# Cross-covariance attention with a multiplicative feed-forward: last outputs that lag, softmax steps closer together, and the first q tile on another DMA queue

## The chip, the cores and the metric

The kernel runs on one core of one Trainium2 chip. The metric is the device time of one execution in microseconds (us). The profile's span leaves some 1.8 us of the measured time out.

## The reference, cut to what matters

```python
B, N, C = 4, 5824, 256                    # q, k, v: [B, N, C], f32; tau = 1
qn = q / (norm(q, axis=1) + 1e-6);  kn = k / (norm(k, axis=1) + 1e-6)
a  = softmax(kn.transpose(0, 2, 1) @ qn / tau)          # [B, 256, 256]
x  = (v @ a).reshape(B * N, C)
out = ((x @ w1) * (x @ w2)) @ w3 @ w_out                # w1, w2: 256 x 1024; w3: 1024 x 1024; w_out: 1024 x 256
```

The kernel never forms x. It folds the attention matrix of a batch into w1 and w2 (`Wf`), multiplies w3 by w_out once (`W_sb`), and then does for each 512 tokens and each of 8 slices: two products from v with `Wf` (a and b), a cast of a by ScalarE, a product a*b by VectorE, and an output product with `W_sb`.

## The kernel before: the parts that the change touches

TensorE works through batches `b`, chunks `c` of 512 tokens (the last one, "small", has 128 tokens and the 64 left over of a batch) and slices `j`. Everything for the next batch (scores, softmax, folds) hangs on an agenda of (time, work), whose clock counts TensorE's columns. `run_due` emits what is due, so a time on the agenda becomes a place in each engine's program.

```python
nc.scalar.preload_act_table_set("natural_log_exp_and_others")      # at the top
...
return (                                                # softmax of a batch after the first: (cost, time, work)
    [(0.0, 0.0, norms), (0.0, 6.0, k_row)]              # norms: all-reduce on GpSimd
    + [(0.0, 6.0 + 1.3 * i, lambda i=i: k_step(i)) for i in range(4)]
    ...
    + [(0.0, 11.3 + 1.3 * ct, lambda ct=ct: scale(ct)) for ct in range(CT)]
    + [(0.0, 12.0 + 1.3 * ct, lambda ct=ct: exps(ct)) for ct in range(CT)]
    + [(0.2, 16.5, sums)]
    + [(0.43, 17.5 + 1.1 * i, lambda i=i: fold(i)) for i in range(8)]
)
...
for nm in "kq":                                         # the first tiles, uncast
    raw[nm] = work.tile([P, half, C], F32, tag="o_sb", name=f"raw_{nm}", bufs=3)
    nc.sync.dma_start(out=raw[nm], in_=qk_main[nm, 0][0][:, :half, :])
    load_part(nm, 0, 0, half, PIECE)                    # the rest: GpSimd's casting loads
...
for jt in range(FT):
    at(26.0 + 1.2 * jt, 0.87, lambda jt=jt: w_unit(jt)) # w3 @ w_out; needs w3 turned by DMA
...
lag = LAG_END if b == B - 1 and c == NCH - 1 else LAG   # 5 or 2: outputs run behind a and b
while w_ready[0] and len(pend) > lag and npop < 2:
    emit_out(*pend.pop(0))
...
while pend:                                             # the end
    emit_out(*pend.pop(0))
```

In `emit_out` the small chunk of an odd batch has two output matmuls per slice, first the leftover rows of both batches, then the main rows. At the last slice ScalarE copies the main rows to SBUF and issues their store, and VectorE copies the leftover rows; the stores of their two halves go by SyncE and, at the very end, by ScalarE.

## Time and profile before

| | value |
|---|---|
| time, median of 3 runs | 571.08 us (570.57 to 572.03) |
| span of the profiled run | 569.5 us |
| TensorE busy, clock | 98%, 1.00 |
| last matmul starts | 565.36 us |
| from there to the end of the span | 4.10 us |

Read it in this order: which engine is busy, then whether its "busy" hides waiting, then where. The lines are in the prediction. One thing to know for its first group of lines: the GB/s of a casting load count the bf16 bytes that it writes (the list of DMA issues has 512 KB for eight tiles of q or k that come by a casting load, and the same 512 KB for four that come uncast). So 211 GB/s in the stage from 6 to 30 us and 418 GB/s of the uncast tiles at 3 us are the same rate of reading.

### The profile page before, as it was taken

The numbers are of one execution on the slowest core, as the hardware profiler recorded it, in microseconds if no ns is written. First come the engines' busy times: TensorE is split into PE (matmuls) and PEld (weight loads), VectorE is DVE, ScalarE is ACT, GpSimd is POOL, SyncE is SP. The second block draws the span as 40 slices with busy tenths as digits, with TensorE's granted clock in tenths as the row PEclk, the third lists the DMA queues.
The fourth block names the chain that finished last, engine by engine and source line by source line (L and its number), as shares of the span: only waits on it lengthen the run. The fifth ranks groups of instructions, "written<-read, shape, count | busy, mean of one in ns | idle before, by whom it ended". The sixth has DMA issues, their size and how long they took to land.

```text
span 569.5 us, 10098 instructions
## 1 busy us (share of the span) xinstructions
PE 558.9 (98%) x3755; PEld 354.9 (62%) x3755; DVE 375.7 (66%) x581; ACT 340.5 (60%) x627; POOL 77.2 (14%) x163
## 2 busy tenths in 40 slices
PE   8799999999999999999999999999999999999997
PEld 5664576776666666666666666666665656656665
DVE  1047645788966577887766567787866665565564
ACT  1057535777766577777675567777756554454453
POOL 4260013020220110121210111030120000000000
PEclk9999999999999999999999999999999999999999
DMA  9999989978455696595761495766740325221011
GB/s 213 211 175 208 168 170 233 225 171 195 112 147 120 132 194 147 98 184 128 148 148 73 95 217 121 155 120 121 184 112 39 85 74 148 63 70 68 38 73 58
DMA packets 75105, 77.45 MB, mean 136 GB/s; under 512 B 54193, under 2 KB 58801, under 8 KB 75057
## 3 DMA queue, kind: packets, MB, share of 16 engines
q0 software_dynamic: 15760, 38.93, 39.1%
q1 hardware_dynamic: 59072, 37.69, 22.3%
q8 instruction: 29, 0.48, 0.3%
q10 hardware_dynamic: 224, 0.20, 0.1%
q14 instruction: 20, 0.16, 0.1%
HBM read 78.91 MB, written 23.86 MB: 180 GB/s over the span
## 4 chain that ended last, share of the span: by engine, by line
PE 91%; DMA 6%; ACT 1%; DVE 1%; POOL 0%; issue 0%; ACTq 0%; POOLq 0%
PE o L519 28%; PE b L477 27%; PE a L477 27%; PE G L193 5%; DMA k<-in_k_dram 5%; PE fold L364 2%; DMA w3T<-w_wout 1%; PE w L643 1%; ACT kr L284 0%; ACT as L483 0%; PE quarter L390 0%; POOL k L112 0%; DVE s L318 0%; ACT e L323 0%; DVE abs L498 0%
## 5 line engine op out<-in xcount | busy, mean ns | idle before, releaser
L498 DVE TENSOR_TENSOR abs<-as,b 128x512 bf16<-128x512 bf16 x336 | 230.2, 686 | 138.0 <-ACT as L483 124.9
L483 ACT CAST as<-a 128x512 bf16<-128x512 f32 (+1 forms) x384 | 216.2, 563 | 173.4 <-DVE abs L498 87.1
L477 PEld LDWEIGHTS <-Wf 128*128 128x128 bf16 x1536 | 148.8, 98 | 101.7 <-issue 1.8
L477 PE MATMUL a<-vT,Wf 128*128 128x512 bf16 x704 | 209.4, 379 | 0.4 <-ACT Wf L399 0.4
L477 PE MATMUL b<-vT,Wf 128*128 128x512 bf16 x704 | 209.4, 379 | 0.0
L519 PE MATMUL o<-W_sb,abs 128*128 128x256 bf16 x1344 | 201.1, 273 | 0.0
L519 PEld LDWEIGHTS <-abs 128*128 128x128 bf16 x1344 | 131.4, 98 | 80.8
L202 DVE TENSOR_TENSOR acc<-acc,sq 128x1024 f32<-128x1024 f32 x66 | 80.4, 1219 | 0.7 <-ACT sq L190 0.7
L193 PE MATMUL G<-k,q 128*128 128x256 bf16 x276 | 49.6, 273 | 0.0
L190 ACT ACTIVATE sq<-q 128x512 f32<-128x512 bf16 x66 | 41.8, 634 | 0.0
L190 ACT ACTIVATE sq<-k 128x512 f32<-128x512 bf16 x66 | 41.6, 630 | 0.0
L465 POOL COPY gate_t<-abs 1x1 bf16<-1x1 bf16 x39 | 9.4, 241 | 170.1 <-DVE abs L498 168.8
L540 DVE COPY osb<-o 128x512 f32<-128x512 f32 x44 | 30.1, 684 | 0.9 <-PE o L519 0.9
L193 PEld LDWEIGHTS <-q 128*128 128x128 bf16 x276 | 27.0, 98 | 3.1
L539 ACT COPY osb<-o 128x512 f32<-128x512 f32 x44 | 25.8, 586 | 3.8 <-PE o L519 1.8
L469 POOL COPY gate_t<-vT 1x1 bf16<-1x1 bf16 x16 | 3.3, 208 | 162.5 <-DMA vT<-v 162.5
L112 POOL DMA_DIRECT2D q<-in_q_dram x28 | 15.1, 539 | 12.5 <-DMA k<-in_k_dram 5.5
L284 ACT ACTIVATE kr<-row 128x256 f32<-128x256 f32 x1 | 0.4, 384 | 26.0 <-PE row L272 26.0
L371 ACT ACTIVATE Wf<-fold,rs 128x512 bf16<-128x512 f32 x15 | 10.3, 688 | 9.0 <-PE fold L364 9.0
L488 DVE TENSOR_TENSOR left<-as,b 128x192 bf16<-128x192 bf16 x32 | 11.2, 353 | 5.7 <-ACT as L483 3.5
L364 PE MATMUL fold<-w,e 128*128 128x512 bf16 x56 | 14.7, 379 | 0.0
L498 DVE TENSOR_TENSOR abq<-as,b 128x512 bf16<-128x512 bf16 x16 | 10.8, 686 | 5.1 <-ACT as L483 4.6
(98 smaller groups left out, 241.8 us busy)
## 6 DMA issues: line engine op xcount, KB each, us to landing
out_dram<-osb SPq DMA_DIRECT2D x44, 512.0 KB, 3.6
k<-in_k_dram POOLq DMA_DIRECT2D x19, 512.0 KB, 8.6
v<-in_v_dram POOLq DMA_DIRECT2D x19, 512.0 KB, 5.2
q<-in_q_dram POOLq DMA_DIRECT2D x18, 512.0 KB, 6.6
w_wout<-in_moe_w_dram POOLq DMA_DIRECT2D x1, 2048.0 KB, 23.1
k<-in_k_dram POOLq DMA_DIRECT2D x4, 320.0 KB, 7.6
v<-in_v_dram POOLq DMA_DIRECT2D x4, 320.0 KB, 5.3
q<-in_q_dram POOLq DMA_DIRECT2D x3, 320.0 KB, 4.3
```

Source lines behind the costliest of these rows:

```text
L112: nc.gpsimd.dma_start(out=pieces[nm, n, pi][:, lo:hi, :], in_=qk_main[nm, n][0][:, pi * PIECE + lo : pi * PIECE + hi, :])
L190: nc.scalar.activation(out=dst[:, :, part, :], in_=src[:, o : o + 2, :], func=AF.Square)
L193: nc.tensor.matmul(G[:, ct, :], lhsT=qt[:, i, ct * P : (ct + 1) * P], rhs=kt[:, i, :], start=(pr == 0 and part == 0 and ct == 0), stop=(pr ...
L202: nc.vector.tensor_add(accs[n], accs[n], sqs[0])
L364: nc.tensor.matmul(m, lhsT=st["e"][:, c2, c1 * P : (c1 + 1) * P], rhs=w12[:, c2, w, lo:hi], start=(c2 == 0), stop=(c2 == CT - 1),)
L477: nc.tensor.matmul(t[:, :n], lhsT=Wf[b][:, ct, w, j * P : (j + 1) * P], rhs=rhs_of(b, c, ct), start=(ct == 0), stop=(ct == CT - 1),)
L483: nc.scalar.copy(a_sb[:, :n], tiles[0][:, :n])
L488: nc.vector.tensor_mul(both, a_sb[:, :n], tiles[1][:, :n])
L498: nc.vector.tensor_mul(ab, a_sb, tiles[1])
L519: nc.tensor.matmul(tl[h][:, o, :], lhsT=lhsT, rhs=W_sb[:, j, :], start=(j == 0 and o == 0), stop=(j == FT - 1 and (small or o == 1)), skip ...
L539: nc.scalar.copy(o[:, 0:2, :], tl[0])
L540: nc.vector.tensor_copy(o[:, 2:4, :], tl[1])
```

## The change

Its intent: take the waits out of a TensorE that is otherwise full. The first q tile no longer queues behind that of k; the products with w3 wait until it has been turned; the softmax steps stand closer, so its folds are over sooner; the lag of the outputs rises gradually ahead of the last chunk; and the leftover rows are finished ahead of the last main rows.

```diff
-    nc.scalar.preload_act_table_set("natural_log_exp_and_others")
...
-            [(0.0, 0.0, norms), (0.0, 6.0, k_row)]
-            + [(0.0, 6.0 + 1.3 * i, lambda i=i: k_step(i)) for i in range(4)]
-            + [(0.0, 6.5, q_sums), (0.0, 9.3, lambda: q_norm(st["ss"]))]
-            + [(0.0, 11.3 + 1.3 * ct, lambda ct=ct: scale(ct)) for ct in range(CT)]
-            + [(0.0, 12.0 + 1.3 * ct, lambda ct=ct: exps(ct)) for ct in range(CT)]
-            + [(0.2, 16.5, sums)]
-            + [(0.43, 17.5 + 1.1 * i, lambda i=i: fold(i)) for i in range(8)]
+            [(0.0, 0.0, norms), (0.0, 5.5, k_row)]
+            + [(0.0, 5.5 + 1.2 * i, lambda i=i: k_step(i)) for i in range(4)]
+            + [(0.0, 6.0, q_sums), (0.0, 8.5, lambda: q_norm(st["ss"]))]
+            + [(0.0, 10.3 + 1.2 * ct, lambda ct=ct: scale(ct)) for ct in range(CT)]
+            + [(0.0, 11.0 + 1.2 * ct, lambda ct=ct: exps(ct)) for ct in range(CT)]
+            + [(0.2, 14.6, sums)]
+            + [(0.43, 15.6 + 1.1 * i, lambda i=i: fold(i)) for i in range(8)]
...
-                nc.scalar.copy(o[:, 0, :], tl[0][:, 0, :])      # emit_out, small chunk: the main rows stood first
-                other = nc.scalar if b == B - 1 else nc.sync
-                other.dma_start(out=rows[:, NT - 1, :], in_=o[:, 0, :])
...
-                    for k, eng in enumerate((nc.sync, other)):
...
+                    for m in (b - 1, b):                        # now both halves of the leftover rows by nc.sync
...
+                if only != 1:                                   # and then the main rows
+                    nc.scalar.copy(o[:, 0, :], tl[0][:, 0, :])
+                    other = nc.scalar if b == B - 1 else nc.sync
+                    other.dma_start(out=rows[:, NT - 1, :], in_=o[:, 0, :])
...
-        nc.sync.dma_start(out=raw[nm], in_=qk_main[nm, 0][0][:, :half, :])
+        first = nc.sync if nm == "k" else nc.scalar
+        first.dma_start(out=raw[nm], in_=qk_main[nm, 0][0][:, :half, :])
         load_part(nm, 0, 0, half, PIECE)
+    nc.scalar.preload_act_table_set("natural_log_exp_and_others")
...
-                at(26.0 + 1.2 * jt, 0.87, lambda jt=jt: w_unit(jt))
+                at(27.5 + 1.2 * jt, 0.87, lambda jt=jt: w_unit(jt))
...
-                lag = LAG_END if b == B - 1 and c == NCH - 1 else LAG
+                lag = LAG
+                if b == B - 1 and c >= NCH - 2:
+                    lag = LAG_END if c == NCH - 1 else LAG + (LAG_END - LAG) * (j + 1) // FT
...
-    while pend:
-        emit_out(*pend.pop(0))
+    n = len(pend)                       # `only`: 1 the leftover rows' matmul of a slice, 0 the main rows'
+    for i, only in [(i, 1) for i in range(n - 1)] + [(i, 0) for i in range(n - 2)] + [(n - 1, 1), (n - 2, 0), (n - 1, 0)]:
+        emit_out(*pend[i], only=only)
```

More of the change, by code (lines that the diff above doesn't have):

```diff
@@ L501, in emit_ab, with emit_out @@
         clock[0] += 4 * (n * MM_COL + MM_FIX)
-    def emit_out(b, c, j, ab):
+    def emit_out(b, c, j, ab, only=None):
         small = c == NCH - 1
@@ L517, in emit_out @@
         for s, lhsT in reversed(list(enumerate(lhs))) if small else enumerate(lhs):
+            if only is not None and s != only:
+                continue
             h, o = (s, 0) if small else divmod(s, 2)
@@ L528, in emit_out @@
             if small:
-                nc.scalar.copy(o[:, 0, :], tl[0][:, 0, :])
-                other = nc.scalar if b == B - 1 else nc.sync
-                other.dma_start(out=rows[:, NT - 1, :], in_=o[:, 0, :])
-                if b % 2 == 1:
+                if b % 2 == 1 and only != 0:
                     o2 = work.tile([P, D], F32, tag="kr", name=f"oleft_{b}", bufs=1)
                     nc.vector.tensor_copy(o2, tl[1][:, 0, :])
-                    for k, eng in enumerate((nc.sync, other)):
-                        m = b - 1 + k
-                        eng.dma_start(out=out[m * N + NT * P : (m + 1) * N, :], in_=o2[k * LEFT : (k + 1) * LEFT, :])
+                    for m in (b - 1, b):
+                        k = (m - b + 1) * LEFT
+                        nc.sync.dma_start(out=out[m * N + NT * P : (m + 1) * N, :], in_=o2[k : k + LEFT, :])
+                if only != 1:
+                    nc.scalar.copy(o[:, 0, :], tl[0][:, 0, :])
+                    other = nc.scalar if b == B - 1 else nc.sync
+                    other.dma_start(out=rows[:, NT - 1, :], in_=o[:, 0, :])
             else:
@@ L541, in emit_out @@
                 nc.sync.dma_start(out=rows[:, 4 * c : 4 * c + 4, :], in_=o)
-            del out_tiles[b, c]
+            if only is None:
+                del out_tiles[b, c]
     NDEF = 4
```

## The prediction

> **What bounds the kernel now.** I read the page first, then the windows table, the chain of waits, the timeline at four places, and the spacing of single matmuls in the trace.
>
> ```profile
> PE 558.9 (98%) x3755; PEld 354.9 (62%) x3755; DVE 375.7 (66%) x581; ACT 340.5 (60%) x627; POOL 77.2 (14%) x163
> PEclk9999999999999999999999999999999999999999
> PE 91%; DMA 6%; ACT 1%; DVE 1%; POOL 0%; issue 0%; ACTq 0%; POOLq 0%
> ```
>
> TensorE is the bound: 98% busy, full clock, 91% of the chain that ended last; DMA has 6% of it, nearly all at the start. A "busy" row hides small idle times, because a matmul's end is modelled and rows overlap. So I went through all matmuls and took from each start-to-start distance the time of its columns at 2.4 per ns (four times that for f32). The sum over the span is 542.4 us of columns and 21.7 us of gaps. By stage: 8.4 us of gaps before 31 us (operands come by DMA), 1.4 us in the first softmax (31 to 37), 1.0 us from 60 to 76, 0.8 us from 177.5 to 181.3, 0.7 us from 559.6 to 563.8. The long stages have 1.5 to 1.8 us per 90 to 110 us, which is a few ns per instruction. After the last matmul the span runs on for almost 4 us. Nothing in the change takes a matmul away that matters, so it can win only in these gaps and in the tail. Four groups of lines show those that it aims at. First the start, timeline and windows (columns of the last: window, length, busy time and count of each engine, clock, DMA share, GB/s):
>
> ```profile
> 0.72 1.28 ACT L73 ACT_TABLE_LOAD   x1 [0.72 <-PEq L741]
> 0.73 0.40 SPq L557 DMA_DIRECT2D raw_k<-in_k_dram  x1
> 1.19 0.41 SPq L557 DMA_DIRECT2D raw_q<-in_q_dram  x1
> ...
> 2.00:2.50 0.50, 0.50 (x3) 0.16 (x2) 0.00 (x0) 0.01 (x1) 0.50 (x2) 1.00 0.63 106
> 2.50:3.00 0.50, 0.50 (x3) 0.23 (x2) 0.00 (x0) 0.00 (x0) 0.50 (x2) 1.00 0.65 229
> 3.00:3.50 0.50, 0.50 (x3) 0.23 (x2) 0.00 (x0) 0.00 (x0) 0.50 (x2) 1.00 1.05 418
> ...
> 6.00:30.00 24.00, 20.13 (x248) 17.09 (x248) 1.00 (x5) 0.63 (x1) 6.36 (x12) 1.00 1.09 211
> ```
>
> To see: the raw q tile is issued 0.46 us after the raw k tile on one queue; DMA reaches its rate only at 3 us, and from there to 30 us it is full. The casting loads' first packet starts at 4.6 us, as the plain ones run dry. Second, the wait for the turned w3 (timeline, TensorE alone):
>
> ```profile
> 63.56 0.59 PE L477 MATMUL b<-vT,Wf 128*128 128x512 bf16 x2
> 64.28 1.05 PE L643 MATMUL w<-w_wout,w3T 128*128 128x256 bf16 x8
> ...
> 67.33 0.59 PE L477 MATMUL b<-vT,Wf 128*128 128x512 bf16 x2
> 68.21 1.05 PE L643 MATMUL w<-w_wout,w3T 128*128 128x256 bf16 x8 [0.29 <-DMA w3T<-w_wout]
> ```
>
> Two 512-column matmuls take 0.43 us from start to start; here it is 0.72 and 0.88, so 0.29 and 0.45 are lost. Third, the end of batch 0, and fourth, the start of the last chunk:
>
> ```profile
> 177.51 0.59 PE L364 MATMUL fold<-w,e 128*128 128x512 bf16 x2
> ...
> 179.12 0.33 PE L477 MATMUL a<-vTt,Wf 128*128 128x192 bf16 x2
> 179.54 0.33 PE L477 MATMUL b<-vTt,Wf 128*128 128x192 bf16 x2
> ```
> ```profile
> 559.93 0.33 PE L477 MATMUL a<-vTt,Wf 128*128 128x192 bf16 x2
> 560.29 0.33 PE L477 MATMUL b<-vTt,Wf 128*128 128x192 bf16 x2
> 560.45 0.33 PE L477 MATMUL a<-vTt,Wf 128*128 128x192 bf16 x2
> ```
>
> Two 192-column matmuls take 0.16 us where nothing waits; these take 0.42 and 0.36.
>
> **What the Trainium skill says.** "Perfetto Trace Analysis", section "Identifying the Most-Contended Engine", says that matmul busy share is no good measure of headroom; this trace agrees (98% busy, yet 21.7 us of gaps). "TensorE: Matmul & The Clock Gate", section "Back-to-back issue gap", gives columns/2.4 + 2.5 ns, some 216 ns for 512 columns; the trace agrees (0.43 us for two). "DMA: Bandwidth & Descriptors", section "Issuing engines are not separate DMA queues", says that a second issuing engine saves only the sequencer's time; here that is the 0.46 us. "ScalarE: Activation LUTs", section "What ACT_TABLE_LOAD costs", has 1283 ns for a table load; the trace has 1.28 us.
>
> **The change part by part.**
>
> First, q's raw tile from ScalarE's queue. ScalarE can issue at 0.72 instead of SyncE at 1.19. Its table load then runs from about 1.15 to 2.45, and ScalarE's first real work, the cast of that tile, was at 5.58: free. The gain is bounded by 0.46 us and needs DMA engines that are not full between 1.75 and 3 us. They are at 0.63 and 0.65 for 1 us, so about 0.36 us of their time is spare. Everything to 30 us follows this transfer at a full DMA rate, and TensorE's end of the first stage follows the last q and k pieces, so what is gained stays. I take 0.3 us.
>
> Second, the products of w3 and w_out start 1.5 us later on the schedule's clock (26.0 to 27.5). A step between them is 0.86 us (four 512-column matmuls), so the first moves one or two steps, from 63.99 (where it would have started) to 64.9 or 65.7; its operand landed at 64.23. The third, which waited for a landing at 68.16, comes 3.5 to 4.3 us behind the first in either case of two folds per step (0.87 + 0.86 us a round), so at 68.3 or later. The other two landings, 69.98 and 71.98, were met already. The work is only moved. Gain 0.29 + 0.45 = 0.74; I take 0.65.
>
> Third, the closer softmax. Its first fold moves from 17.5 to 15.6, so 1.9 us earlier, one or two steps of 1.3 us. In batch 0 the last two of eight folds now fall into the small chunk (from 175.55), where a step is only 0.44 us of TensorE, and their evictions on ScalarE (0.69 us) and VectorE (0.75 us) hold the small casts and products up. The six steps from 177.94 to 181.32 take 3.38 us; undisturbed 6 x 0.44 = 2.64. Loss 0.74 us. One step earlier already puts all folds ahead of it. In batches 1 and 2, where they do lie ahead, this chunk loses 0.06 and up to 0.33 us. So gain 0.74 - 0.2 = 0.5 us in batch 0, and about nothing in the others.
>
> Fourth, the last outputs. The lag now rises from 2 to 5 over the chunk before the last, so the last chunk's first three steps have four 256-column output matmuls (0.43 us) each between them, instead of none. From 559.60 to 561.35 TensorE did four steps with no outputs: 1.75 us for 4 x 0.33 = 1.32, so 0.43 lost, and all of it should go. A gap of 0.18 us at 562.88 (an output bank that waits for its copy to SBUF) stays, as the same output step still precedes it. The outputs' number is the same. The new order at the end finishes the leftover rows two matmuls (0.22 us) before the last one instead of one (0.11): 0.11 us sooner to their copy. Before, the last issue was ScalarE's at 566.52, and landed 2.0 us later; now both leftover transfers go by SyncE, the second some 0.5 us after the first (0.49 us each), so near 566.40. Gain 0.12. Together 0.5 us.
>
> Sum: 0.3 + 0.65 + 0.5 + 0.5 = 1.95 us. Of 571.08 this leaves 569.1.
>
> **The rivals.** (a) The closer softmax blocks ScalarE. In batch 0 the all-reduce ran from 154.70 to 157.94, and the first Ln on its result started at 158.37, only 0.43 us later. Moved by 0.5 us of clock it has about 0.5/1.3 = 0.4 chance of falling one step (1.3 us) earlier; ScalarE would then stand for 0.87 us, and with two pairs of PSUM tiles TensorE may lose 0.2 to 0.5. Batches 1 and 2 have 1.96 us there. In batch 2 ScalarE already stood 1.09 us twice for VectorE's scaled scores, and TensorE lost 0.27 at 428.5; the pattern may change for better or worse by as much in each batch. This alone would make the time 569.4 to 569.9. (b) The start gains nothing: the two tiles share one set of DMA engines, k lands later as q lands sooner, and the casting loads begin as before. For it: the slow first 1 us may be the first packets' latency rather than lack of work. The time would be 569.4. (c) The later w3 products save nothing, if their transposes slip too or TensorE then meets a wait at another place: 569.8. (d) The tail gains only its stalls, since what lands last is fixed by a slow 2 us transfer: 569.2.
>
> **Range and chances.** All parts right with the full 0.46 and 0.74: 568.6. Rivals (a) to (c) together: about 570.6. The three runs of before spread over 1.5 us, so a median of such runs may lie 0.4 off. I say 569.1, and 568.1 to 570.3 eight times in ten. Two per cent are 11.4 us, more than all the gaps that the change touches, so "same" is nearly sure.
>
> **What would show each step.** Start: ScalarE issues raw_q at about 0.72, DMA share from 2 to 3 us rises above 0.65, and the last q piece lands before 32.3 by 0.2 to 0.46. Products: no wait between b (L477) and w above 0.1 us. Softmax: all folds of batch 0 ahead of its small chunk, whose steps take 0.44 us. Tail: alternating a, b, o rows from the first small step; the last transfer is SyncE's leftover. Wrong if the gaps come back elsewhere, above all on ScalarE near the all-reduce, or if the time is above 570.3.

## The result, and the profile after

The changed kernel took 569.67 us (median of 6 runs, 569.33 to 570.51) against 571.32 us for the kernel before in the same rounds (6 runs, 570.57 to 572.03). Ratios are the mean time of one kernel's runs over that of the other's of the same rounds, so not quite the ratio of the medians: 0.9973, with a 95% interval of 0.9960 to 0.9986. That is 0.27%, or 1.5 us, and within the 2% that count as "same". The time lies in the predicted range.

From the page of the changed kernel:

```profile
PE 557.6 (98%) x3755; PEld 355.4 (63%) x3755; DVE 375.4 (66%) x581; ACT 338.7 (60%) x627; POOL 77.9 (14%) x163
PE 93%; DMA 5%; ACT 1%; POOL 0%; issue 0%; DVE 0%; ACTq 0%; POOLq 0%
```

The span fell from 569.5 to 567.7. I went through the starts of all matmuls again, as for the prediction. The last matmul starts at 563.39 us instead of 565.36, so 1.97 us sooner, and from there to the end it takes 4.29 us instead of 4.10. All figures in this table but those of the last row are gaps on TensorE, in us, beyond the time of the columns:

| stage | before | after | difference |
|---|---|---|---|
| 0 to 37 us: loads of q and k, first softmax | 9.76 | 9.78 | 0 |
| 37 to 60 | 0.66 | 0.53 | -0.13 |
| 60 to 76: products with w3 | 1.01 | 0.26 | -0.75 |
| 160 to 175: softmax in batch 0 | 0.32 | 0.46 | +0.14 |
| 175 to 182.5: small chunk of batch 0 | 0.89 | 0.36 | -0.53 |
| 420 to 438: softmax in batch 2 | 0.62 | 0.36 | -0.26 |
| 552 to the last matmul | 0.86 | 0.41 | -0.45 |
| last matmul to the end | 4.10 | 4.29 | +0.19 |

The start. The first three rows are from the timeline (ScalarE's queue is ACTq), the next from the windows table, as in the prediction:

```profile
0.73 0.40 SPq L562 DMA_DIRECT2D raw_k<-in_k_dram  x1
0.73 0.40 ACTq L562 DMA_DIRECT2D raw_q<-in_q_dram  x1
5.66 0.69 DVE L580 CAST k<-raw_k 128x1024 bf16<-128x1024 f32 x1 [3.87 <-DMA raw_k<-in_k_dram]
...
2.00:2.50 0.50, 0.50 (x3) 0.16 (x2) 0.00 (x0) 0.44 (x1) 0.50 (x2) 1.00 0.63 123
2.50:3.00 0.50, 0.50 (x3) 0.23 (x2) 0.00 (x0) 0.00 (x0) 0.50 (x2) 1.00 0.77 238
3.00:3.50 0.50, 0.50 (x3) 0.22 (x2) 0.00 (x0) 0.00 (x0) 0.50 (x2) 1.00 0.99 401
```

Both transfers are issued at 0.73, and yet DMA moves 123 and 238 GB/s where it moved 106 and 229. The k tile lands at 5.63 us instead of 4.35 and its cast starts at 5.66 instead of 4.38; the q tile lands at 5.47 instead of 5.56. The last q piece of the stage lands at 32.29 us, before at 32.31. The other traces tell the same: with the two tiles on two queues k lands at 5.39 to 5.75 us and q at 5.46 to 5.91 (six traces); with both on one queue k lands at 4.33 to 4.72 and q at 5.54 to 5.93 (eight). Side by side, each of the two takes about as long as both took in line.

The products with w3, timeline of TensorE:

```profile
65.16 0.60 PE L476 MATMUL b<-vT,Wf 128*128 128x512 bf16 x2
65.59 1.04 PE L649 MATMUL w<-w_wout,w3T 128*128 128x256 bf16 x8
...
66.90 0.59 PE L476 MATMUL b<-vT,Wf 128*128 128x512 bf16 x2
67.33 1.91 PE L649 MATMUL w<-w_wout,w3T 128*128 128x256 bf16 x16
```

From b to w it is now 0.43 us both times, which is the time of b itself. Both waits are gone.

The small chunk of batch 0 (its a and b rows begin at 175.67), and the first steps of the last chunk:

```profile
174.81 1.03 PE L363 MATMUL fold<-w,e 128*128 128x512 bf16 x4
...
178.08 0.33 PE L476 MATMUL a<-vTt,Wf 128*128 128x192 bf16 x2
178.38 0.33 PE L476 MATMUL b<-vTt,Wf 128*128 128x192 bf16 x2
```
```profile
556.75 0.33 PE L476 MATMUL a<-vTt,Wf 128*128 128x192 bf16 x2
556.92 0.33 PE L476 MATMUL b<-vTt,Wf 128*128 128x192 bf16 x2
557.08 0.60 PE L521 MATMUL o<-W_sb,abs 128*128 128x256 bf16 x4
```

The last folds of batch 0 now stand ahead of its small chunk, where one gap of 0.13 us (178.08 to 178.38, against 0.16 undisturbed) is the largest that is left. In the last chunk each a and b is followed by four output matmuls, with no gap.

The end, the timeline of before and then of after:

```profile
566.01 0.49 SPq L537 DMA_DIRECT2D out_dram<-oleft  x1
566.07 0.41 ACTq L531 DMA_DIRECT2D out_dram<-osb  x1
566.52 0.53 ACTq L537 DMA_DIRECT2D out_dram<-oleft  x1
```
```profile
563.93 1.13 SPq L536 DMA_DIRECT2D out_dram<-oleft  x2
564.10 0.36 ACTq L540 DMA_DIRECT2D out_dram<-osb  x1
```

Counted from the start of the last matmul, the three stores were issued at 0.65, 0.71 and 1.17 us and landed at 2.68, 2.51 and 3.18. Now they are issued at 0.54, 0.71 and 1.09, two of them sooner, and land at 2.86, 3.20 and 3.37. Every one of them takes longer, and the span ends 0.92 us after the last landing both times.

### The profile page after: what moved, and what is told of

Read it like the earlier page. It is cut to its first block, busy times and chain, and to the rows that moved or that the text cites. A ratio compares the mean times of both kernels' runs of the same rounds, so it can differ in the third digit from the quotient of the medians.

```text
span 567.7 us, 10095 instructions
## 1 busy us (share of the span) xinstructions
PE 557.6 (98%) x3755; PEld 355.4 (63%) x3755; DVE 375.4 (66%) x581; ACT 338.7 (60%) x627; POOL 77.9 (14%) x163
## 4 chain that ended last, share of the span: by engine, by line
PE 93%; DMA 5%; ACT 1%; POOL 0%; issue 0%; DVE 0%; ACTq 0%; POOLq 0%
PE o L521 28%; PE b L476 28%; PE a L476 28%; PE G L192 5%; DMA k<-in_k_dram 5%; PE fold L363 2%; PE w L649 1%; ACT kr L283 0%; PE quarter L389 0%; POOL k L111 0%; POOL q L111 0%; PE sqk L225 0%; PE row L271 0%; ACT e L322 0%; ACT Wf L398 0%
```

## The experiments

The theory after the comparison: three parts pay what their gaps were worth (products, softmax, lag), the first part pays nothing (theory A below: the start is bound by DMA as a whole; theory B: it does pay 0.3 us), and the new order at the end costs 0.19 us. The rivals: the first part does pay and something hides it; the closer softmax only works by one of its halves; the longer tail comes from elsewhere.

Twelve kernels ran beside the kernel before, on four chips; only kernels of one block of equal "before" times share a chip and its rounds. All gave correct results. "Tail" is the time from the last matmul's start to the end of the span, in the one run of each kernel whose trace was kept.

| kernel | median us | before, same rounds | ratio, 95% interval | last matmul | tail |
|---|---|---|---|---|---|
| first part only | 570.34 | 570.32 | 1.0001 (0.9989 to 1.0014) | 565.19 | 4.08 |
| all but the first part | 569.46 | 570.32 | 0.9984 (0.9972 to 0.9997) | 563.76 | 4.28 |
| table load ahead of the transfer | 569.48 | 570.32 | 0.9981 (0.9968 to 0.9995) | 563.51 | 4.29 |
| later products only | 571.07 | 570.32 | 1.0012 (0.9999 to 1.0024) | 564.72 | 4.07 |
| closer softmax only | 570.69 | 570.81 | 0.9997 (0.9984 to 1.0011) | 564.48 | 4.11 |
| sums and folds only | 571.65 | 570.81 | 1.0012 (0.9998 to 1.0026) | 565.90 | 4.08 |
| the rest of the softmax only | 570.59 | 570.81 | 0.9998 (0.9984 to 1.0011) | 564.67 | 4.09 |
| rising lag only | 570.50 | 570.81 | 0.9994 (0.9981 to 1.0006) | 564.85 | 4.09 |
| before again | 571.29 | 571.04 | 0.9998 (0.9985 to 1.0011) | 565.54 | 4.07 |
| all but the order at the end | 569.48 | 571.04 | 0.9972 (0.9958 to 0.9985) | 563.51 | 4.05 |
| leftover rows by one transfer | 572.04 | 571.04 | 1.0017 (1.0004 to 1.0030) | 563.34 | 6.74 |
| last stores on three queues | 575.83 | 570.97 | 1.0081 (1.0067 to 1.0095) | 564.79 | 10.39 |

The kernel before, run against itself, has an interval of 0.13% either way, or 0.7 us. No single part is clearly worth more. So the verdicts on the parts rest on gaps in the traces; the times only tell the whole change, or most of it, from the kernel before. From 76 us on the gaps repeat to 0.02 us from trace to trace wherever the schedule is the same, which makes this possible. In some traces 7 of the 3755 matmul records are missing: three of the idle warm-up matmuls at the start, and one fold (512 columns, 0.21 us) in each batch; where one falls into a stage that I quote, I have taken it off the gaps. The first 76 us are another matter: there the gaps depend on when each load lands, and that differs from run to run.

### The first part alone

```diff
-    nc.scalar.preload_act_table_set(...)       # at the top
+        first = nc.sync if nm == "k" else nc.scalar
...
+    nc.scalar.preload_act_table_set(...)       # after the two loads
```

> Only the first part: the raw q tile from ScalarE's queue, ahead of its table. Theory A (the start is set by slow first packets, then by a full DMA): as in the changed kernel, DMA moves 123, 123, 238 GB/s in the half microseconds from 1.5 to 3, the last q piece lands at 32.3 us, the columns' gaps before 37 us stay at 9.8 us, and the time is that of before within 0.3 us. Theory B (the earlier issue does win 0.3 us, which the changed kernel hid): the last q piece lands near 32.0 and the time falls by 0.3 us.

The last q piece landed at 32.30 us, as before, the gaps before 37 us are 9.78 (missing records taken off), and the time is the same to 0.1 us. That is what theory A expects. DMA moved 147, 139 and 279 GB/s, somewhat more than the 123, 123 and 238 expected, and yet the stage ended no sooner. But one trace and a time good to 0.7 us do not rule out 0.3 us; the next section puts all traces together.

### All but the first part

The changed kernel with these lines as they were.

> The changed kernel with the first part undone (both raw tiles from SyncE, the table at the top). Theory A: the whole gain stays; last matmul at 563.4 us, span 567.7, the time 1.5 to 1.8 us under before. Theory B: 0.3 us of it is lost.

The time is 0.16% under before, or 0.9 us where 1.5 to 1.8 were expected (the interval reaches 1.6), with the table load's variant beside it at 0.19%, so the two can't be told apart. The last matmul is at 563.76 in this trace, 0.37 us later than in the changed kernel's; the last q piece landed at 32.52 here, 0.23 us later than there, and lies anywhere from 32.02 to 32.83 in the traces of all kernels, whichever queue the raw q tile had. So this one trace says nothing against theory A. All fourteen traces together say more. The first product of v (`a`), which starts when the stage of the loads is over, comes at 37.28 us on average in the six with the first part (37.11 to 37.44) and at 37.40 in the eight without it (37.15 to 37.64). The difference is 0.12 us, with a 95% interval of -0.05 to 0.28. Up to 3 us DMA has moved 237 KB on average with the first part and 228 KB without. So theory B's 0.3 us is not there; whether 0 or 0.1 us is won, these traces can't tell.

### Table load ahead of the transfer

```diff
+    nc.scalar.preload_act_table_set("natural_log_exp_and_others")    # back at the top
...
-    nc.scalar.preload_act_table_set("natural_log_exp_and_others")    # after the loads
```

> The changed kernel with ScalarE's table load put ahead of its raw q transfer again, so this is issued about 1.3 us later, near 2.0 us. Theory A: the casting loads that queue from 2.4 us fill the DMA engines in its place, so the last q piece still lands within 0.2 us of 32.3 and the time stays within 0.3 us of the changed kernel's (1.5 to 1.8 us under before); only the first products of q may come later. Theory B (the order of issue matters at the start): the last piece lands about 0.5 us or more later and half a microsecond of the gain is lost.

The time stayed, but the experiment did not do what I meant it to do. The timeline of this kernel:

```profile
0.73 1.28 ACT L73 ACT_TABLE_LOAD   x1 [0.73 <-PEq L751]
0.76 0.39 ACTq L563 DMA_DIRECT2D raw_q<-in_q_dram  x1
```

I expected the transfer to be issued at 2.0. It is issued at 0.76, while the table load runs until 2.01: the sequencer of ScalarE hands the load to the engine and goes on. So moving the table load behind the transfer was worth 0.03 us of issue time, and whether a late q tile would hurt was not tested.

### Later products only

```diff
-                at(26.0 + 1.2 * jt, 0.87, lambda jt=jt: w_unit(jt))
+                at(27.5 + 1.2 * jt, 0.87, lambda jt=jt: w_unit(jt))
```

> Only the second part: the products of w3 and w_out 1.5 us later on the schedule's clock. Theory: both waits for the turned w3 (0.29 and 0.45 us) go and nothing takes their place: last matmul at about 564.6 us instead of 565.36, the time 0.6 to 0.8 us under before. Rival: the wait comes back behind the products or at the later turned pieces (landing 69.98 and 71.98), and under 0.3 us is won.

In the trace both waits for the turned w3 are gone and the gaps from 60 to 76 us are 0.26, as in the changed kernel; the last matmul is at 564.72. The time, though, is 0.12% above before, where 0.1% less was expected, and the interval leaves that out. I can't explain it from the one trace, which is of the fastest of its five runs (570.56 us, and before had a median of 570.32); the other four ran up to 1.06 us longer. That the products pay is shown by the gap that went; that they pay in this kernel's mean time is not.

### Before again

> The kernel before, unchanged, run as if it were another: how far two loads of one kernel lie apart, and what its trace shows on this chip. Both theories: ratio 1.000 with an interval that holds it; from 76 us on the same gaps as in the first trace of before (0.53 us more at batch 0's small chunk and 0.26 us more ahead of batch 2's folds than in the changed kernel, 4.1 us from the last matmul to the end); only the wait for the turned w3 at 64 to 68 us, 0.74 us in the first trace, may be another (0.2 to 0.7 us in the other kernels that kept its schedule).

The ratio is 0.9998, and from 76 us on the gaps are those of the first trace of before. The interesting part is the wait for w3. The waits view of this run, TensorE, 37 to 76 us (columns: who waited for whom, us in total, times, longest):

```profile
PE tr_I-615_616 L135 <- DMA v<-in_v_dram: 0.7, 1, 0.7
PE a L477 <- ACT Wf L399: 0.4, 1, 0.4
```

Here a piece of v landed late, TensorE stood 0.84 us from 44.88, and so it came to w3 late enough to wait there for only 0.05 us. The gaps from 37 to 76 us are 1.68 us against 1.67 in the first trace. The loads of one DMA stage end at a time of their own, and TensorE meets them at one place or another. Over all traces these gaps are 1.67, 1.68, 1.49, 1.57, 1.46, 1.71 and 1.07 us with the old time of the products (mean 1.52), and 0.79, 0.85, 0.77, 0.79, 1.07, 0.80 and 1.99 with the new one (mean 1.01). The last of these, the kernel with three queues, again met a piece of v late. So the part is worth 0.75 us in the pair that was compared, and about 0.5 us on average of seven traces each.

### Closer softmax only

The seven softmax lines of the diff, nothing else.

> Only the third part: the closer softmax. Theory: the folds of batch 0 lie ahead of its small chunk, whose gaps fall by 0.53 us; in batch 2 the gap of 0.21 us ahead of the folds goes; in batch 0 a new one of 0.14 us comes near 165. Sum 0.6 to 0.7 us. Rival (blocked ScalarE): under 0.3 us is left.

All three gaps came as expected: 0.36 us at batch 0's small chunk, 0.36 in batch 2, 0.46 from 160 to 175. That is 0.65 us of TensorE's time. The measured time shows 0.03%, with an interval that holds 0.65 us (0.11%).

### Sums and folds only

```diff
-            + [(0.2, 16.5, sums)]
-            + [(0.43, 17.5 + 1.1 * i, lambda i=i: fold(i)) for i in range(8)]
+            + [(0.2, 14.6, sums)]
+            + [(0.43, 15.6 + 1.1 * i, lambda i=i: fold(i)) for i in range(8)]
```

> Of the closer softmax only its last two lines: the sums and the eight folds 1.9 us earlier, all that goes before them as it was. If the folds' evictions in the small chunk are what cost batch 0 its time: the gap there falls by 0.5 us as in the whole change, the gap of 0.21 us in batch 2 stays, and no new gap of 0.14 us comes near 165; the time 0.5 us under before. If it is the steps ahead of the folds that matter, batch 0 keeps its gaps of 0.8 us and nothing is won.

The gap in batch 0's small chunk went, 0.89 to 0.36, as expected of the folds, and nothing new came near 165. But in batch 2 the gaps rose from 0.62 to 1.35 us, which I had not expected. The timeline shows it:

```profile
426.64 0.60 PE L519 MATMUL o<-W_sb,abs 128*128 128x256 bf16 x4
427.57 0.19 PE L341 MATMUL sum<-ones_b,e 128*128 128x1 bf16 x2 [0.33 <-DVE s L318]
428.11 0.20 PE L341 MATMUL sum<-ones_b,e 128*128 128x1 bf16 x2 [0.36 <-ACT e L323]
```

TensorE reaches the sums before the exponentials are there, and stands twice. The folds can only come sooner if the steps ahead of them do.

### The rest of the softmax only

The other five lines of the softmax, with sums and folds at their old times.

> The complement: all steps of the closer softmax but the sums and folds, which stay at their old times. By the same theory batch 0 keeps its gaps of 0.8 us at the small chunk, the gap of 0.21 us in batch 2 goes, the new one of 0.14 us near 165 comes: the time 0.1 us under before, so no difference that can be told.

As expected: 0.89 at batch 0's small chunk, 0.37 in batch 2, 0.46 near 165, and no difference in time. Together the two halves show how the gain comes about. The folds win 0.53 us in batch 0. The steps ahead of them win 0.26 in batch 2, lose 0.14 in batch 0, and are needed in batch 2, where the earlier folds alone cost 0.73 us.

### Rising lag only

```diff
-                lag = LAG_END if b == B - 1 and c == NCH - 1 else LAG
+                lag = LAG
+                if b == B - 1 and c >= NCH - 2:
+                    lag = LAG_END if c == NCH - 1 else LAG + (LAG_END - LAG) * (j + 1) // FT
```

> Of the fourth part only the lag that rises over the chunk before the last; the order of the last outputs as before. Theory: the two gaps of 0.20 us in the last chunk's first steps go, the one of 0.18 (an output bank) stays; last matmul 0.45 us earlier, the time from the last matmul to the end as before, 4.1 us: the time 0.45 us under before. Rival: the steps without outputs in the chunk before stall instead, and nothing is won.

The gaps from 552 us on fell from 0.86 to 0.43, the gap of 0.18 stayed, and the tail is 4.09. The ratio is 0.9994 (0.3 us), with an interval that also holds 1. The rival's stalls in the chunk before do not appear.

### All but the order at the end

The changed kernel with `emit_out` and the last loop as before.

> The changed kernel with the old order of the last outputs and the old queues of their transfers; the lag still rises. Theory: the new order is a loss, as the last transfer lands 3.37 us after the last matmul instead of 3.18 in every trace so far; so the last matmul stays at its place, the time from it to the end falls from 4.29 to 4.1 us, and the time is 0.2 us under the changed kernel's. Rival: the longer landing comes from elsewhere in the change; then 4.29 us stay.

The timeline of the end, last matmul at 563.51:

```profile
564.16 0.49 SPq L536 DMA_DIRECT2D out_dram<-oleft  x1
564.22 0.38 ACTq L530 DMA_DIRECT2D out_dram<-osb  x1
564.64 0.54 ACTq L536 DMA_DIRECT2D out_dram<-oleft  x1
```

The last matmul stayed at its place, the stores land at 2.66, 2.46 and 3.12 us again, and the tail fell to 4.05. The nine traces with the old order have tails of 4.05 to 4.11 us, the three with the changed kernel's order and queues 4.28 or 4.29. So the new order and the new queues together cost 0.2 us; which of the two does was not tested. Its ratio to before, 0.9972, is that of the changed kernel in its own rounds, 0.9973: the time cannot show so little.

### Leftover rows by one transfer

```diff
-                    for m in (b - 1, b):
-                        k = (m - b + 1) * LEFT
-                        nc.sync.dma_start(out=out[m * N + NT * P : (m + 1) * N, :], in_=o2[k : k + LEFT, :])
+                    both = out.rearrange("(n r) c -> n r c", n=B)[b - 1 : b + 1, NT * P :, :]
+                    nc.sync.dma_start(out=both, in_=o2)
```

> The changed kernel with both halves of the leftover rows stored by one transfer of SyncE's instead of two. Theory (plain transfers of SyncE and ScalarE get their descriptors one after the other, some 0.35 us each, so the third one is what lands last): the copies come as before, the second transfer (ScalarE's) starts moving at about 2.0 us after the last matmul and lands at some 3.0 instead of 3.2, nothing comes behind it, and the time from the last matmul to the end falls from 4.29 to about 3.9 us. Rival (what lands last is ruled by a fixed time of a write of some 2.3 to 2.5 us): ScalarE's transfer still lands at 3.2 and the tail is 4.1.

A clear miss, and slower: the tail is 6.74 us. The DMA line of this run from 560 to 571 us in 40 slices (the 512 KB of the chunk before, ScalarE's main rows, then the leftover rows alone):

```profile
GB/s 0 0 0 0 0 0 0 0 223 447 432 432 372 0 0 0 0 26 365 104 7 19 52 45 45 34 52 45 52 45 52 11 0 0 0 0 0 0 0 0
```

The leftover rows move at some 45 GB/s instead of several hundred. The Trainium skill, "DMA: Bandwidth & Descriptors", section "Why a DMA increments its semaphore by 16 and not by 1", says that a transfer is split over the largest number of DMA engines up to 16 that divides the outermost dimension of both sides; the outermost dimension of this store is the 2 batches. The trace agrees: two semaphore packets at its end, where each of the two stores of 64 rows had 16. The part of the expectation about ScalarE's store can be read all the same. With the second store of SyncE gone, it started moving 1.57 us after the last matmul and landed at 2.41, instead of 2.03 and 3.20. That is not what was expected either (2.0 and 3.0): it moved ahead of SyncE's store (first packet at 1.9), which had been issued 0.17 us sooner. So the two start some 0.35 us apart here too, but not in the order of their issue.

### Last stores on three queues

```diff
+                    last_o2[0] = o2
...
-                        nc.sync.dma_start(out=out[m * N + NT * P : (m + 1) * N, :], in_=o2[k : k + LEFT, :])
+                        if only is None or m < b:
+                            nc.sync.dma_start(out=out[m * N + NT * P : (m + 1) * N, :], in_=o2[k : k + LEFT, :])
...
-                    other = nc.scalar if b == B - 1 else nc.sync
+                    other = nc.gpsimd if b == B - 1 else nc.sync
                     other.dma_start(out=rows[:, NT - 1, :], in_=o[:, 0, :])
+                    if only == 0:
+                        nc.scalar.dma_start(out=out[b * N + NT * P : (b + 1) * N, :], in_=last_o2[0][LEFT:, :])
```

> The changed kernel with its three last transfers on three queues: first half of the leftover rows by SyncE, the main rows by GpSimd ([...]its loads in the first trace of before that met an idle queue moved data 1.22 us after the issue), the second half by ScalarE after its copy. Theory (the descriptors of SyncE's and ScalarE's transfers are made one after the other, some 0.35 us each): only two stand in that line now, so ScalarE's half starts moving at about 2.03 us after the last matmul as the second one did, GpSimd's near 1.95, all land by 3.0, and the time from the last matmul to the end is 3.8 to 3.95 us instead of 4.29 (and 4.07 in the old order); everything ahead of the last matmul as in the changed kernel. Rival (GpSimd's path lands later than 3.2, or all three share the same end): 4.1 us or more.

Half right, and by far the slowest. SyncE's store started moving 1.69 us after the last matmul and ScalarE's at 2.00, as expected of two that get their descriptors in turn; they landed at 2.53 and 2.79. GpSimd's was issued only at 0.98:

```profile
565.77 0.55 POOL L543 DMA_DIRECT2D out_dram<-osb  x1 [71.49 <-ACT osb L541]
```

It started moving at 2.31 (1.95 was expected) and landed at 3.12. So all three had landed sooner than the last one of the changed kernel (3.37). But GpSimd's closing drain, recorded from 0.95 us after the last matmul, ended only at 9.60, and the whole program waits for it. The gain of a quarter of a microsecond on the stores was paid for with 6 us. The other traces have the same drain: it takes 8.65 to 8.68 us in all fourteen, and starts with GpSimd's last transfer. Elsewhere that is a load of v near 493 us, and the drain is over by 503, hidden behind TensorE's work; here it starts 0.95 us after the last matmul. So it is not this store that makes the drain long, only its place that exposes it. What the drain does in this time, no trace says. No version that beats the changed kernel clearly was found; the one without the new order is 0.24 us better in its trace's tail, and level with it in time.

## Why the prediction was right, and where it was not

It said 569.1 us with a range of 568.1 to 570.3; the measured time is 569.67. It named a gain of 1.95 us; the traces of the pair show 1.77 us of span and the times 1.5 us. The sum came near partly by luck, because errors of both signs cancelled.

**The bound** was right: TensorE's columns are the same to 0.1 us, and all that changed are its gaps and the tail. One reading of the skill was short: the 216 ns that "TensorE: Matmul & The Clock Gate", section "Back-to-back issue gap", gives for 512 columns are for an isolated matmul, and for a stream of them the section has some 131 ns. The streams of this trace have 216 ns from start to start, so here the measurement decides for the longer time. The count of columns takes the six f32 matmuls (518 columns in all) at four times the time, where the trace has 0.32 us for 256 of them; that moves some 0.2 us between columns and gaps, in both kernels alike.

**The start, 0.3 us, was wrong**; rival (b) was right. The step that failed: "They are at 0.63 and 0.65 for 1 us, so about 0.36 us of their time is spare." With two transfers in line from the beginning the shares are 0.63 and 0.77, the rate up to 3 us is that of before to 20 GB/s, and the first packet of the second transfer (here k's) moves at 2.13 us against 1.75 for the first. A lack of work in line was not what kept DMA slow. The Trainium skill, "DMA: Bandwidth & Descriptors", section "Queues, rings and completion order", says that SyncE's and ScalarE's queues have no descriptor generator of their own; the 0.38 us between two transfers issued in the same instant agrees with it, and so do the 0.34 and 0.31 us between the first two stores of the end. It does not explain why the first packets are slow (a median of 524 ns each from 1.7 to 2.0 us before, 248 in the changed kernel, 159 ns from 2.5 on in both), nor why DMA moves 123 GB/s from 1.5 to 2 us with either; that stays open.

**The products, 0.65 us, were right** in mechanism and step count: w starts at 65.59, one of the two times named (65.7), with no wait. The pair shows 0.75; the mean of all traces is nearer to 0.5, since a late piece of v can take the wait's place. That was rival (c) in part.

**The softmax, 0.5 us, was right in batch 0** (0.53). "About nothing in the others" missed batch 2's 0.26. The other half of rival (a) came true in a small way: not at the all-reduce, which kept its 0.44 us ahead of the first Ln (157.05 and 157.49), but at the scaled scores, for which ScalarE stood 1.09 us in batch 0; TensorE lost 0.14 near there.

**The lag, 0.43 us, was right** (0.45, and the gap of 0.18 stays). **The order, 0.12 us, was wrong in sign**: it lost 0.19. The failed step is not the issue ("the second some 0.5 us after the first (0.49 us each), so near 566.40"): counted from the last matmul, the last one did come 0.08 us sooner. It is that the landing was left at 2.0 us behind it: the landings took 2.28 to 2.49 us instead of 1.80 to 2.03. In the old order the 128 main rows moved first (from 1.62 us) and the leftover rows behind them; in the new one the leftover rows move first (from 1.69), with data packets of 67, 81 and 162 ns in the median of each 0.2 us from 1.6 to 2.2, where the main rows' had 46, and the main rows start only at 2.03. That order and queues of the three together are what costs is shown by the experiment; why the packets of the first store are slower is not.

Adding it up by stage: 0 + 0.75 + 0.65 + 0.45 - 0.19 = 1.66 us, and 0.13 us from 37 to 60 us, where a piece of v happened to land sooner, make 1.79, the 1.77 of the spans within rounding.

## What to carry to other kernels

When the busiest engine is 98% busy, sum the gaps between its starts by stage and predict from those; here such sums gave three of the five parts to within 0.15 us. Judge parts worth less than the noise by gaps that repeat from trace to trace, and run the old kernel against itself to learn what the noise is. A DMA share below 1 is no proof that the DMA engines lack work: from 2.0 to 2.5 us it was 0.63 with the first two tiles on one queue and with them on two, and the second queue brought no gain. A store at the very end is judged by its landing, not by its issue, and what GpSimd does last by the drain that follows it.

## What the Trainium skill lacked or had wrong

- "DMA: Bandwidth & Descriptors", section "Issuing engines are not separate DMA queues", says that a second issuing engine saves the sequencer's time. Lacking: how far apart the two then move. For two transfers issued in the same instant the first packets came 0.38 us apart (1.75 and 2.13 us; 0.41 to 0.78 in the other five traces), and the 0.46 us saved at the issue brought no gain that fourteen traces could tell from 0.
- The same page, section "Queues, rings and completion order", has the DMA engines take turns between queues that have work. Packets of the two uncast tiles from SyncE's and ScalarE's queues did take turns from 3 to 4.5 us in the changed kernel. But in the first trace of before the casting loads issued from 1.22 us on moved no packet until 4.62 (4.60 to 4.93 in all traces), when the uncast ones began to run dry; later, on an idle queue, the first packet came 1.22 us after the issue. Whether their descriptors were ready sooner at the start, no trace shows.
- "ScalarE: Activation LUTs", section "What ACT_TABLE_LOAD costs", has the load's 1283 ns (1.28 us here). Lacking on that page: a DMA issue behind it in ScalarE's program does not wait for it (issued at 0.76 us, the load running from 0.73 to 2.01).
- No page warns of a transfer of GpSimd's shortly before the end of a program: the drain that closes GpSimd's part took 8.65 to 8.68 us in all fourteen traces, and where it followed a last store it ended 9.6 us after the last matmul, 6.5 us after the data had landed.
